# A 3008-point FFT filter ahead of a squared-ReLU FFN: filter loaded as quadrants, zero matmuls in the prologue, two loads of batch 2 later

## The chip, the cores and the metric

The kernel runs on one core of a Trainium2 chip. The metric is the device time of one launch in microseconds (us), the median of three runs. Beside it one execution was profiled, and all rows below are of that execution. [...]

## The reference

```python
X = np.fft.rfft(x, axis=1)                 # x: 8 batches x 3008 rows x 256 columns
F = (filt_r + 1j * filt_i)[None, :, :]     # 1505 frequencies x 256 columns
y = np.fft.irfft(X * F, n=3008, axis=1)    # 8 x 3008 x 256
h = np.maximum(y.reshape(24064, 256) @ w_in, 0.0)    # w_in: 256 x 2048
out = h * h @ w_out                                  # w_out: 2048 x 256
```

All inputs and the output are f32.

## The kernel before

A 3008-point transform is split as 64 x 47. For each batch there are four stages. Stage A (`unit_a`, for batch 0 `chunk_a0`) multiplies by the 47-point matrix; its result u goes through DRAM (`dU`, written in four chunks by `write_u`, read back by `read_u` as the tile ut) so that rows change places. Stage B (`unit_b`, 12 units of two of the 24 columns c) multiplies by `sSB` into psB, and VectorE multiplies psB with the filter sF into prod. Stage P (`unit_p`) multiplies by `sSP` (for batch 0 also by `sSPx`, sSP with its halves exchanged), ScalarE copies the result to ze, and four writes take it to DRAM (`dZ`). Stage Y (`read_z`, then 16 `unit_y`) reads it back as zt and makes yt, the columns of y. The FFN runs over 47 groups of 512 rows, each of 8 slots; a slot has four 512-wide matmuls (`ffn_g1`, psH, ReLU to h on ScalarE L402), the square on VectorE (`ffn_sq`, L406) and eight 256-wide matmuls of the group before (`ffn_g2`, psO).

The order of the work is the order of the program text on every engine and every DMA queue (`manual_schedule`); a DMA issued by an engine stands in that engine's order, and what waits holds back all that follows on the same engine or queue. Batches 1 to 7 are laid between the FFN slots by `fft_plan(b)`: `put(r, place, ...)` puts a step into slot r of the batch's plan, after the first (place 0) or the second (place 1) set of matmuls. For batch 1 the plan's slot 0 is FFN slot 0. Batch 0 is the prologue and has no FFN to lie beside.

In the prologue SP issues three loads of x (L184, 1 MB each), the filter (L193, two loads of 1.5 MB), sSB and sSP (L197, L199), and later ut and the two weight matrices (`load_w`). ACT issues the writes of u and ze, the reads of zt and the first two loads of batch 1. POOL issues no DMA. The tile of each filter part has 128 partitions: quadrant q (32 partitions) holds 12 of the 24 columns, and quadrants 0 and 3 together are the first half of the columns, 1 and 2 the second. `cast_f(im, q, engine)` casts a quadrant into sF, and `cross_f(im, k)` copies or negates half k across partitions on VectorE. The tiles of u have three buffers (`p_u`), so the copies of the fourth chunk of batch 0 (L289, L291) wait until the first chunk's write has landed.

The order of the prologue is L468 to L514: casts of x, four chunks of stage A, ut, weights, casts of the filter, copies of sSPx on POOL, crosses, then 12 turns of stages B and P, casts of the weights on POOL (`cast_w`), reads of zt, stage Y. The FFN begins after it. The filter's load before is

```python
src = bass.AP(tensor=filt.tensor, offset=filt.offset,
              ap=[[12 * D, 4], [47 * D, 32], [1, 12 * D]])
nc.sync.dma_start(out=t, in_=src)
```

whose outermost dimension has 4 entries.

Of the kernel before, what the change touches and what calls it, by code (L numbers as in the profile page):

```python
# [9 lines left out]
F16 = mybir.dt.float16  # L10
F32 = mybir.dt.float32
# [85 lines left out]
def kernel(  # L97
# [9 lines left out]
    nc = tc.nc  # L107
    B, S, D = x.shape
# [13 lines left out]
    const = ctx.enter_context(tc.tile_pool(name="const", bufs=1))  # L122
# [10 lines left out]
    p_y = ctx.enter_context(tc.tile_pool(name="p_y", bufs=2))  # L133
# [12 lines left out]
    def psO(name):  # L146
        return pps.tile([128, 2, 256], F32, tag="psO", name=name, bufs=2)

    def psH(name):
        return pps.tile([128, 2, 512], F32, tag="psH", name=name, bufs=2)  # L150
# [27 lines left out]
    x0 = []  # L178
    v0 = xrows[0:2048, :].rearrange("(p m) d -> p m d", m=16)
    v1 = xrows[2048:3072, :].rearrange("(p m) d -> p m d", m=8)  # L180
    for k, v in enumerate((v0[:, 0:8, :], v1, v0[:, 8:16, :])):
        t = (p_h2 if k == 2 else p_x32).tile([128, 8, D], F32, tag="h2" if k == 2 else "x32",
                                             name=f"x0_{k}")
# [1 line left out]
        x0.append(t)  # L185


    f32s = []
    for k, filt in enumerate((filt_r, filt_i)):
        t = p_y.tile([128, 12, D], F32, tag="yt", name=f"f32_{k}")  # L190
        src = bass.AP(tensor=filt.tensor, offset=filt.offset,
                      ap=[[12 * D, 4], [47 * D, 32], [1, 12 * D]])
        nc.sync.dma_start(out=t, in_=src)  # L193
        f32s.append(t)

    sSB = const.tile([128, NC, 128], F16, name="sSB")
    nc.sync.dma_start(out=sSB, in_=dSB.ap().rearrange("p (a b) -> p a b", b=128))  # L197
    sSP = const.tile([128, NC, 128], F16, name="sSP")
    nc.sync.dma_start(out=sSP, in_=dSP.ap().rearrange("p (a b) -> p a b", b=128))  # L199


    sF = const.tile([128, 2, NC, D], F16, name="sF")

    def cast_f(im, q, eng):

        o = 64 * im + 32 * (q // 2)
        c0 = (0, 12, 12, 0)[q]
        src = f32s[im][32 * q:32 * q + 32, :, :]
        if q >= 2:
            src = src[:, ::-1, :]  # L210
        dst = sF[o:o + 32, im, c0:c0 + 12, :]
        if eng is nc.scalar:
            eng.mul(out=dst, in_=src, mul=-1.0 if im else 1.0)  # L213
        elif im:
            eng.tensor_scalar_mul(out=dst, in0=src, scalar1=-1.0)
        else:
            eng.tensor_copy(out=dst, in_=src)

    def cross_f(im, k):
        c = slice(12 * k, 12 * k + 12)  # L220
        if im:
            nc.vector.tensor_scalar_mul(out=sF[0:64, 1, c, :], in0=sF[64:128, 1, c, :],  # L222
                                        scalar1=-1.0)
        else:
            nc.vector.tensor_copy(out=sF[64:128, 0, c, :], in_=sF[0:64, 0, c, :])  # L225
# [5 lines left out]
    def load_w():  # L231
        w32 = p_h2.tile([128, 2, DFF], F32, tag="h2", name="win32")
        nc.sync.dma_start(out=w32, in_=moe_w_in.rearrange("(t r) j -> r t j", r=128))
        o32 = p_h2.tile([128, NJT, 256], F32, tag="h2", name="wout32")
        nc.sync.dma_start(out=o32, in_=moe_w_out.rearrange("(jt r) c -> r jt c", r=128))
        w32s.extend([w32, o32])

    def cast_w():
        w32, o32 = w32s
        for k in range(4):  # L240
            nc.gpsimd.tensor_copy(out=sWin[:, :, 512 * k:512 * k + 512],
                                  in_=w32[:, :, 512 * k:512 * k + 512])
        for k in range(4):
            nc.gpsimd.tensor_copy(out=sWout[:, 4 * k:4 * k + 4, :], in_=o32[:, 4 * k:4 * k + 4, :])
# [30 lines left out]
    def chunk_a0(c):  # L275

        us[(0, c)] = p_u.tile([96, 8, D], F16, tag="u", name=f"u_0_{c}")
        for k in range(2):
            ps = psH(f"psA_0_{c}_{k}")
            for i in range(2):  # L280
                m = slice(4 * k + 2 * i, 4 * k + 2 * i + 2)
                nc.tensor.matmul(ps[0:96, i, :], s0[:, c // 2, :], x016[2 * (c % 2)][:, m, :],
                                 start=True, stop=False)
                nc.tensor.matmul(ps[0:96, i, :], s0[0:120, 2 + c, :], x016[1][0:120, m, :],
                                 start=False, stop=True)
            o = us[(0, c)][:, 4 * k:4 * k + 4, :]
            pv = ps[0:96].rearrange("p t (a d) -> p (t a) d", d=D)
            if k == 0:
                nc.scalar.copy(out=o, in_=pv)  # L289
            else:  # L290
                nc.vector.tensor_copy(out=o, in_=pv)  # L291
        write_u(0, c, nc.scalar)

    def read_u(b):
        ut = p_ut.tile([128, NC, D], F16, tag="ut", name=f"ut_{b}")
        v = dU[b].rearrange("(p s) d -> p s d", s=NC)
        for s0, s1 in ((0, 8), (8, 24)):
            nc.sync.dma_start(out=ut[:, s0:s1, :], in_=v[:, s0:s1, :])
        uts[b] = ut
# [27 lines left out]
    def unit_p(b, p):  # L327
        c, i6 = divmod(p, 3)
        if i6 == 0:
            zes[(b, c)] = p_ze.tile([128, 6, D], F16, tag="ze", name=f"ze_{b}_{c}")  # L330
        prod = prods.pop((b, p))
        ps = psO(f"psP_{b}_{p}").rearrange("p a d -> p (a d)") if prologue[0] else psF(f"psP_{b}_{p}")
        for i in range(2):
            c2 = 2 * p + i
            if b == 0:
                for v, w in enumerate((sSP, sSPx[0])):
                    nc.tensor.matmul(ps[:, i * D:(i + 1) * D], w[:, c2, :], prod[:, v, i, :],
                                     start=(v == 0), stop=(v == 1))
            else:
                nc.tensor.matmul(ps[:, i * D:(i + 1) * D], sSP[:, c2, :], prod[:, i, :],  # L340
                                 start=True, stop=True)
        nc.scalar.copy(out=zes[(b, c)][:, 2 * i6:2 * i6 + 2, :],  # L342
                       in_=ps.rearrange("p (a d) -> p a d", d=D))
        if i6 == 2:
            q = nc.scalar if prologue[0] else nc.sync
            q.dma_start(
                out=dZ[b].rearrange("(p s) d -> p s d", s=NC)[:, 6 * c:6 * c + 6, :],
                in_=zes.pop((b, c)))
# [76 lines left out]
    def fft_plan(b):  # L425

        plan = {}

        def put(r, place, f, *a):
            plan.setdefault((r, place), []).append((f, a))  # L430

        if b == 1:
            for c in range(2):
                put(c, 1, cast_x, b, c)
                put(c, 1, load_x, b, c + 2)
                put(5 + 2 * c, 1, cast_x, b, c + 2)
        for a in range(16):
            r = 2 + a // 2 + (a >= 8) if b == 1 else a // 2
            put(r, a % 2, unit_a, b, a)
        put(11 if b == 1 else 8, 1, read_u, b)  # L440
        for p in range(12):
            r = 15 + p if b == 1 else 13 + 19 * p // 11
            put(r, 0, unit_b, b, p)
            put(r + (b == 1), b == 1, unit_s, b, p)
            put(r + 2 + (b == 1), 1, unit_p, b, p)
        for c in range(4):
            put(30 if b == 1 else 35, 1, read_z, b, c)
        if b + 1 < B:
            for c in range(2):
                put(22, 1, load_x, b + 1, c)  # L450
            for c in range(4):
                put(27 + 3 * c, 1, cast_x, b + 1, c)
                if c < 2:
                    put(27 + 3 * c, 1, load_x, b + 1, c + 2)
        for n in range(16):
            if b == 1:
                r, k = divmod(n, 3) if n < 6 else divmod(n - 2, 2)
                put(33 + r, min(k, 1), unit_y, b, n)
            else:
                put(39 + n // 2, n % 2, unit_y, b, n)  # L460
        return plan
# [18 lines left out]
        cast_x0(2, i, nc.scalar.copy)  # L480
    chunk_a0(1)
    chunk_a0(3)
    read_u(0)
    load_w()
    for q in (0, 3):
        cast_f(0, q, nc.scalar)
    for q in (1, 2):
        cast_f(0, q, nc.gpsimd)
    for q in (0, 3):
        cast_f(1, q, nc.vector)  # L490
    for q in (1, 2):
        cast_f(1, q, nc.scalar)

    sSPx.append(p_x32.tile([128, NC, 128], F16, tag="x32", name="sSPx"))
    for k in range(2):
        c = slice(12 * k, 12 * k + 12)
        nc.gpsimd.tensor_copy(out=sSPx[0][0:64, c, :], in_=sSP[64:128, c, :])
        nc.gpsimd.tensor_copy(out=sSPx[0][64:128, c, :], in_=sSP[0:64, c, :])
    for k in range(2):
        for im in range(2):  # L500
            cross_f(im, k)
    for r in range(14):
        if r < 12:
            unit_b(0, r)
        if r >= 2:
            unit_p(0, r - 2)
    cast_w()
    for c in range(4):
        read_z(0, c)
# [1 line left out]
        load_x(1, c, q=nc.scalar)  # L511
    for n in range(16):
        unit_y(0, n)
    prologue[0] = False  # L514

    work = {}
# [5 lines left out]
    for s in range((NG + 1) * SLOTS):  # L522
        g, k = divmod(s, SLOTS)
# [40 lines left out]
```

## Time and profile before

| | us |
|---|---|
| runs | 852.3, 854.63, 855.31; median 854.63 |
| the profiled execution's own time | 851.58 |
| its span (first to last instruction) | 849.5 |
| PE busy in the span | 770.7 (91%) |
| DVE, ACT, POOL busy | 552.1, 553.9, 40.6 |
| first matmul of the FFN (L398) | at 97.69 |

Times in rows are microseconds from the span's start. PE is TensorE's matmuls, PEld its weight loads, DVE VectorE, ACT ScalarE, POOL GpSimd, SP the queue engine that issues most DMAs; "SPq" and "ACTq" mark DMA issues. Batch 0 fills the first 97 us, and nothing of the FFN can run before it; from about 190 us on, TensorE is busy all the time.

### The profile page before, as it was taken

The numbers are of one execution on the slowest core, as the hardware profiler recorded it, in microseconds if no ns is written. First come the engines' busy times: TensorE is split into PE (matmuls) and PEld (weight loads), VectorE is DVE, ScalarE is ACT, GpSimd is POOL, SyncE is SP. The second block draws the span as 40 slices with busy tenths as digits, with TensorE's granted clock in tenths as the row PEclk, the third lists the DMA queues.
The fourth block names the chain that finished last, engine by engine and source line by source line (L and its number), as shares of the span: only waits on it lengthen the run. The fifth ranks groups of instructions, "written<-read, shape, count | busy, mean of one in ns | idle before, by whom it ended". The sixth has DMA issues, their size and how long they took to land.

```text
span 849.5 us, 13895 instructions
## 1 busy us (share of the span) xinstructions
PE 770.7 (91%) x5800; PEld 538.7 (63%) x5800; DVE 552.1 (65%) x862; ACT 553.9 (65%) x697; POOL 40.6 (5%) x42
## 2 busy tenths in 40 slices
PE   3105699899999999999999999999999999999998
PEld 1003356566767766677677767677777767676666
DVE  2028479655996579855995579755995579544332
ACT  2035476667777767777777767776777767766664
POOL 0215006200000000000000000000000000000000
PEclk9557599989999999999999999999999999999999
DMA  9328955545455245815455235815454242511111
GB/s 269 96 91 328 221 173 157 135 102 152 144 140 149 81 131 142 204 57 174 125 144 137 82 130 149 208 61 168 129 144 123 81 144 81 130 35 42 38 38 50
DMA packets 89366, 110.10 MB, mean 130 GB/s; under 512 B 3936, under 2 KB 79328, under 8 KB 84704
## 3 DMA queue, kind: packets, MB, share of 16 engines
q1 hardware_dynamic: 82088, 102.71, 41.6%
q10 hardware_dynamic: 7216, 6.51, 3.0%
q8 instruction: 45, 0.74, 0.4%
q14 instruction: 17, 0.14, 0.1%
HBM read 59.40 MB, written 49.81 MB: 129 GB/s over the span
## 4 chain that ended last, share of the span: by engine, by line
PE 84%; DMA 7%; DVE 4%; issue 2%; ACT 2%; ACTq 0%; SPq 0%; DVEq 0%
PE psO L413 38%; PE psH L398 37%; DMA dU<-u 5%; PE psA L264 3%; PE psY L368 2%; PE psB L304 2%; PE psP L340 2%; DVE prod L307 2%; DMA zt<-dZ 1%; DMA x<-in_x_dram 1%; ACT h L402 1%; ACT sF L213 1%; DVE yf L322 0%; DVE sF L225 0%; DVE sF L222 0%
## 5 line engine op out<-in xcount | busy, mean ns | idle before, releaser
L402 ACT ACTIVATE h<-psH 128x1024 f16<-128x1024 f32 x376 | 385.1, 1025 | 191.9 <-PE psH L398 190.4
L398 PE MATMUL psH<-yt,sWin 128*128 128x512 f16 (+7 forms) x1728 | 389.7, 354 | 0.4 <-ACT yt L375 0.2
L413 PE MATMUL psO<-sWout,h 128*128 128x256 f16 x3008 | 390.0, 273 | 0.0
L413 PEld LDWEIGHTS <-h 128*128 128x128 f16 x3008 | 291.4, 98 | 77.8 <-issue 0.6
L406 DVE TENSOR_TENSOR h<-h 128x1024 f16<-128x1024 f16 x376 | 258.9, 697 | 107.6 <-ACT h L402 107.2
L398 PEld LDWEIGHTS <-sWin 128*128 128x128 f16 x1728 | 160.3, 98 | 102.9 <-issue 4.8
L307 DVE TENSOR_TENSOR prod<-psB,sF 128x1024 f16<-128x1024 f32 x96 | 116.1, 1219 | 4.1 <-PE psB L304 3.3
L304 PE MATMUL psB<-ut,sSB 128*128 128x256 f16 x192 | 37.9, 281 | 47.5 <-DMA ut<-dU 41.9
L377 DVE CAST yt<-psY 128x376 f16<-128x376 f32 x64 | 35.2, 550 | 68.1 <-PE psY L368 67.8
L342 ACT CAST ze<-psP 128x512 f16<-128x512 f32 x96 | 56.2, 585 | 28.7 <-PE psP L340 17.8
L271 DVE CAST u<-psA 96x512 f16<-96x512 f32 x56 | 38.4, 686 | 47.8 <-PE psA L264 47.7
L304 PEld LDWEIGHTS <-sSB 128*128 128x128 f16 x192 | 19.2, 100 | 71.0 <-DMA sSB<-cSB 33.8
L420 ACT COPY ost<-psO 128x512 f32<-128x512 f32 x94 | 55.4, 590 | 6.7 <-PE psO L413 6.0
L368 PEld LDWEIGHTS <-zt 96*128 96x128 f16 x512 | 36.5, 105 | 27.9 <-DMA zt<-dZ 13.9
L368 PE MATMUL psY<-sC,zt 96*128 96x94 f16 x512 | 43.2, 217 | 12.0 <-DMA zt<-dZ 12.0
L264 PE MATMUL psA<-x,sC 94*96 94x512 f16 x112 | 42.3, 382 | 0.8 <-ACT u L269 0.6
L375 ACT CAST yt<-psY 128x376 f16<-128x376 f32 x64 | 29.9, 468 | 15.6 <-PE psY L368 15.6
L322 DVE TENSOR_TENSOR yf<-prod,yf 128x512 f16<-128x512 f16 x84 | 35.5, 423 | 3.0 <-POOL yf L316 0.5
L251 DVE CAST x<-x 94x2048 f16<-94x2048 f32 x28 | 34.1, 1217 | 2.1 <-DMA x<-in_x_dram 2.1
L289 ACT CAST u<-psA 96x1024 f16<-96x1024 f32 x4 | 4.0, 1007 | 44.6 <-DMA dU<-u 32.3
L269 ACT CAST u<-psA 96x512 f16<-96x512 f32 x56 | 32.2, 574 | 0.0
L340 PE MATMUL psP<-yf,sSP 128*128 128x256 f16 x168 | 32.1, 273 | 0.0
(31 smaller groups left out, 185.6 us busy)
## 6 DMA issues: line engine op xcount, KB each, us to landing
out_dram<-ost SPq DMA_DIRECT2D x94, 256.0 KB, 3.8
x<-in_x_dram SPq DMA_DIRECT2D x22, 768.0 KB, 5.8
dU<-u SPq DMA_DIRECT2D x28, 384.0 KB, 3.5
dZ<-ze SPq DMA_DIRECT2D x28, 384.0 KB, 2.5
zt<-dZ SPq DMA_DIRECT2D x28, 384.0 KB, 5.4
ut<-dU SPq DMA_DIRECT2D x8, 1024.0 KB, 5.9
ut<-dU SPq DMA_DIRECT2D x8, 512.0 KB, 3.7
x<-in_x_dram SPq DMA_DIRECT2D x3, 1024.0 KB, 8.1
```

The costliest lines, as they stand in the source:

```text
L264: nc.tensor.matmul(ps[0:96, :], sSA, x16s[(b, c)][:, 2 * i:2 * i + 2, :], start=True, stop=True)
L271: nc.vector.tensor_copy(out=o, in_=pv)
L304: nc.tensor.matmul(ps[:, i * D:(i + 1) * D], sSB[:, 2 * p + i, :], uts[b][:, 2 * p + i, :], start=True, stop=True)
L307: nc.vector.tensor_mul(out=prod, in0=ps.rearrange("p (a d) -> p a d", d=D).unsqueeze(1).to_broadcast([128, 2, 2, D]), in1=sF[:, :, 2 * p:2 ...
L340: nc.tensor.matmul(ps[:, i * D:(i + 1) * D], sSP[:, c2, :], prod[:, i, :], start=True, stop=True)
L342: nc.scalar.copy(out=zes[(b, c)][:, 2 * i6:2 * i6 + 2, :], in_=ps.rearrange("p (a d) -> p a d", d=D))
L368: nc.tensor.matmul(ps[:, 94 * jj:94 * jj + 94], zt[:, 4 * (g % 2) + jj, dt * 128:(dt + 1) * 128], sSY, start=True, stop=True)
L398: nc.tensor.matmul(ps[:, i, o:o + n], sWin[:, dt, jt * 128:(jt + 1) * 128], yts[b][:, dt, r:r + n], start=(dt == 0), stop=(dt == 1))
L402: nc.scalar.activation(out=h2[:, 2 * s:2 * s + 2, :], in_=ps, func=AF.Relu)
L406: nc.vector.tensor_mul(out=v, in0=v, in1=v)
L413: nc.tensor.matmul(pso[g][:, t % 2, :], h2s[g][:, jt, t * 128:(t + 1) * 128], sWout[:, jt, :], start=(jt == 0), stop=(jt == NJT - 1))
L420: nc.scalar.copy(out=ost, in_=pso[g])
```

## The change

The filter is loaded as eight quadrant loads of 32 partitions, 384 KB each, whose outermost dimension has 32 entries. Quadrants 0 go on SP where the whole loads stood, quadrants 3 on POOL behind a copy of one element per partition from the second tile of x, quadrants 1 on SP behind the reads of ut, and quadrants 2 on POOL. `keep_warm(n)` issues n matmuls of 128x512 zeros on zeros: 14 ahead of stage A, 50 behind it, 24 ahead of stage Y and two behind every second unit of stage Y. The casts of the second half of the filter move behind the first turns of stages B and P: two on POOL behind the copies of sSPx, two on ACT in turns 2 and 4, and the two crosses of the second half into turn 4. In the plan of batch 1, the four casts of batch 2's x move from slots 27, 30, 33, 36 to 31, 33, 35, 37, and its last two loads from slots 27 and 30 to 31 and 33.

```diff
--- before.py
+++ after.py
@@ -185,18 +185,35 @@
         x0.append(t)
 
 
-    f32s = []
-    for k, filt in enumerate((filt_r, filt_i)):
-        t = p_y.tile([128, 12, D], F32, tag="yt", name=f"f32_{k}")
-        src = bass.AP(tensor=filt.tensor, offset=filt.offset,
-                      ap=[[12 * D, 4], [47 * D, 32], [1, 12 * D]])
-        nc.sync.dma_start(out=t, in_=src)
-        f32s.append(t)
-
+    f32s = [p_y.tile([128, 12, D], F32, tag="yt", name=f"f32_{k}") for k in range(2)]
+
+    def load_f(im, q, eng):
+        filt = filt_i if im else filt_r
+        src = bass.AP(tensor=filt.tensor, offset=filt.offset + 12 * q * D,
+                      ap=[[47 * D, 32], [1, 12 * D]])
+        eng.dma_start(out=f32s[im][32 * q:32 * q + 32].rearrange("p a d -> p (a d)"), in_=src)
+
+    load_f(0, 0, nc.sync)
+    load_f(1, 0, nc.sync)
     sSB = const.tile([128, NC, 128], F16, name="sSB")
     nc.sync.dma_start(out=sSB, in_=dSB.ap().rearrange("p (a b) -> p a b", b=128))
     sSP = const.tile([128, NC, 128], F16, name="sSP")
     nc.sync.dma_start(out=sSP, in_=dSP.ap().rearrange("p (a b) -> p a b", b=128))
+
+    nc.gpsimd.tensor_copy(out=f32s[0][96:128, 0, 0:1], in_=x0[1][96:128, 0, 0:1])
+    load_f(0, 3, nc.gpsimd)
+    load_f(1, 3, nc.gpsimd)
+
+
+    zero = const.tile([128, 512], F16, name="zero")
+    nc.vector.memset(zero, 0.0)
+
+    def keep_warm(n, y=False):
+        ps = psH("warm")[:, 0, :] if y else psO("warm").rearrange("p a d -> p (a d)")
+        for _ in range(n):
+            nc.tensor.matmul(ps, zero[:, 0:128], zero, start=True, stop=True)
+
+    keep_warm(14)
 
 
     sF = const.tile([128, 2, NC, D], F16, name="sF")
@@ -449,9 +466,10 @@
             for c in range(2):
                 put(22, 1, load_x, b + 1, c)
             for c in range(4):
-                put(27 + 3 * c, 1, cast_x, b + 1, c)
+                r = 31 + 2 * c if b == 1 else 27 + 3 * c
+                put(r, 1, cast_x, b + 1, c)
                 if c < 2:
-                    put(27 + 3 * c, 1, load_x, b + 1, c + 2)
+                    put(r, 1, load_x, b + 1, c + 2)
         for n in range(16):
             if b == 1:
                 r, k = divmod(n, 3) if n < 6 else divmod(n - 2, 2)
@@ -480,30 +498,38 @@
         cast_x0(2, i, nc.scalar.copy)
     chunk_a0(1)
     chunk_a0(3)
+    keep_warm(50)
     read_u(0)
+    for im in range(2):
+        load_f(im, 1, nc.sync)
     load_w()
     for q in (0, 3):
         cast_f(0, q, nc.scalar)
-    for q in (1, 2):
-        cast_f(0, q, nc.gpsimd)
     for q in (0, 3):
         cast_f(1, q, nc.vector)
-    for q in (1, 2):
-        cast_f(1, q, nc.scalar)
+    for im in range(2):
+        cross_f(im, 0)
+    for im in range(2):
+        load_f(im, 2, nc.gpsimd)
 
     sSPx.append(p_x32.tile([128, NC, 128], F16, tag="x32", name="sSPx"))
     for k in range(2):
         c = slice(12 * k, 12 * k + 12)
         nc.gpsimd.tensor_copy(out=sSPx[0][0:64, c, :], in_=sSP[64:128, c, :])
         nc.gpsimd.tensor_copy(out=sSPx[0][64:128, c, :], in_=sSP[0:64, c, :])
-    for k in range(2):
-        for im in range(2):
-            cross_f(im, k)
+    for q in (1, 2):
+        cast_f(0, q, nc.gpsimd)
     for r in range(14):
         if r < 12:
             unit_b(0, r)
         if r >= 2:
             unit_p(0, r - 2)
+        if r in (2, 4):
+            cast_f(1, r // 2, nc.scalar)
+        if r == 4:
+            cross_f(0, 1)
+            cross_f(1, 1)
+    keep_warm(24, True)
     cast_w()
     for c in range(4):
         read_z(0, c)
@@ -511,6 +537,8 @@
         load_x(1, c, q=nc.scalar)
     for n in range(16):
         unit_y(0, n)
+        if n % 2:
+            keep_warm(2, True)
     prologue[0] = False
 
     work = {}
```

## Rows read from the trace of the kernel before

**Rows 1.** Stretches: length, PE, PEld, DVE, ACT, POOL busy (count), clock, DMA share, GB/s.

```profile
0.00:10.00 10.00, 0.58 (x1) 0.31 (x2) 1.99 (x4) 1.28 (x1) 0.20 (x4) 1.00 0.83 307
...
30.00:40.00 10.00, 0.00 (x0) 0.00 (x0) 0.00 (x0) 0.00 (x0) 2.42 (x1) 0.50 0.25 87
...
90.00:100.00 10.00, 8.04 (x70) 5.84 (x71) 5.14 (x9) 4.12 (x9) 0.00 (x0) 0.50 1.11 235
...
200.00:400.00 200.00, 200.00 (x1548) 141.93 (x1547) 145.37 (x240) 143.97 (x185) 0.00 (x0) 1.00 0.48 134
```

**Rows 2.** Who waited for whom up to 130 us: total, times, longest.

```profile
PE psB L304 <- DMA ut<-dU: 41.9, 1, 41.9
POOL sF L217 <- DMA f<-in_filt_r_dram: 37.1, 1, 37.1
...
PEld L368 <- DMA zt<-dZ: 9.0, 4, 7.4
```

**Rows 3.** The chain that ended last: start, length, what.

```profile
14.55 38.93 DMA dU<-u
...
69.15 1.94 DVE prod L307 x2
...
88.28 7.69 DMA zt<-dZ
...
97.69 5.12 PE psH L398 x12
...
105.12 0.88 PE psH L398 x4
...
169.00 1.71 PE psO L413 x8
...
176.05 0.87 PE psO L413 x8
```

**Rows 4.** Groups by line, 50 to 90 us: busy us, mean ns, idle before.

```profile
L307 DVE TENSOR_TENSOR prod<-psB,sF 128x1024 f16<-128x1024 f32 x12 | 13.8, 1218 | 0.0
L213 ACT ACTIVATE sF<-f 32x3072 f16<-32x3072 f32 x4 | 11.0, 2760 | 2.5 <-issue 2.4
...
L342 ACT CAST ze<-psP 128x512 f16<-128x512 f32 x12 | 7.0, 586 | 9.1 <-PE psP L337 9.0
...
L497 POOL COPY sSPx<-sSP 64x1536 f16<-64x1536 f16 x2 | 3.5, 1768 | 17.1 <-DMA sSP<-cSP 17.0
L215 DVE TENSOR_SCALAR sF<-f 32x3072 f16<-32x3072 f32 x2 | 3.5, 1754 | 1.1 <-DMA f<-in_filt_i_dram 1.0
L225 DVE COPY sF<-sF 64x3072 f16<-64x3072 f16 x2 | 3.4, 1714 | 3.2 <-ACT sF L213 3.1
L222 DVE TENSOR_SCALAR sF<-sF 64x3072 f16<-64x3072 f16 x2 | 3.1, 1529 | 0.1
...
L291 DVE CAST u<-psA 96x1024 f16<-96x1024 f32 x1 | 1.2, 1221 | 30.7 <-DMA dU<-u 30.7
```

**Rows 5.** Instructions in order of time, 0 to 60 us.

```profile
24.23 0.38 PE L284 MATMUL psA<-x,sC 120*96 120x512 f16 x1
37.58 5.51 POOL L217 CAST sF<-f 32x3072 f16<-32x3072 f32 x2 [37.14 <-DMA f<-in_filt_r_dram]
```

**Rows 6.** DMA issues by line (page, part 6): count, KB, median us to landing.

```profile
x<-in_x_dram SPq DMA_DIRECT2D x22, 768.0 KB, 5.8
dU<-u SPq DMA_DIRECT2D x28, 384.0 KB, 3.5
dZ<-ze SPq DMA_DIRECT2D x28, 384.0 KB, 2.5
...
ut<-dU SPq DMA_DIRECT2D x8, 512.0 KB, 3.7
```

**Rows 7.** Instructions in order of time, SP's queue and PE, 155 to 170 us.

```profile
157.12 0.33 SPq L163 DMA_DIRECT2D x<-in_x_dram  x1
...
159.23 0.32 SPq L346 DMA_DIRECT2D dZ<-ze  x1
164.56 2.38 SPq L353 DMA_DIRECT2D zt<-dZ  x4
...
168.50 0.50 PE L368 MATMUL psY<-sC,zt 96*128 96x94 f16 x4 [3.85 <-DMA zt<-dZ]
```

## The prediction, made before the changed kernel ran

> **What bounds the kernel now.** I began with busy time by stretch [rows 1]. From 200 to 400 us TensorE is busy 200 of 200 us at clock 1.00: nothing in this change makes the FFN itself shorter. In the prologue it is the other way round: between 30 and 40 us no engine but POOL does anything (2.42 us), the DMA engines are busy 0.25 and move 87 GB/s, against 0.83 and 307 GB/s in the first 10 us. A quarter of 16 engines is four, and the filter's load has 4 as its outermost dimension. So the prologue waits for two transfers of 1.5 MB that use four DMA engines.
>
> The waits say who suffers [rows 2]: POOL waits 37.1 us for the filter, and TensorE 41.9 us for ut. The chain shows why ut is late too [rows 3]: the write of the first chunk of u is issued at 14.55 and lands 38.93 us later, where the same write takes 3.5 us at the median later on [rows 6]. It lies behind the filter on those four engines. The last matmul of stage A ran at 24.23 [rows 5], but the copy of its result had to wait 30.7 us [rows 4] for the buffer that this write holds. ut is there only at 24.6 + 41.9 = 66.5, the first product comes at 69.15, the 12 products take 13.8 us [rows 4], to 82.9, and the FFN begins at 97.69 [rows 3]. What the prologue loses, the end loses: the FFN that follows is full.
>
> **The change part by part.** *ut.* The first loads, with 128 outermost, kept 0.83 of the engines busy [rows 1]; with 32 outermost I take a quadrant to spread over all 16. Rate: 307 GB/s at a share of 0.83 [rows 1] is 370 GB/s for a full share. Ahead of or beside the writes of u lie constants and x (3.4 MB), six quadrants (2.4 MB, those on POOL among them) and sSB and sSP (1.6 MB): 7.3 MB, 20 us, so drained at about 21. Stage A's matmuls end at 24.6 [rows 5]; some 16 of them ran at 1.2 GHz, worth 0.427 - 0.22 = 0.21 us each (5.12 / 12 and 0.88 / 4 [rows 3]), 3.4 us if all are at 2.4 GHz. With the last copy (1.22 [rows 4]) the last write is issued at 22.5 to 26; I take 23, since the 14 zero matmuls, 6 us even at 0.427, end at about 7, before the first cast of x. The fill of the zero tile on DVE and the small copy on POOL lie in the wait for x; only POOL's loads stand behind that copy. It lands 3.5 later [rows 6], at 26.5, and the first part of ut 3.7 after that [rows 6], at 30.2.
>
> *First half of the filter.* On ACT, behind the last chunk, two casts of 2.76: 23.4 to 28.9; on DVE two of 1.75 beside them, then crosses of 1.71 and 1.53 [rows 4]: 32.2. TensorE runs 50 zero matmuls from about 21.5; at 0.22 they end at 32.5. First product about 33, instead of 69.15: the zero matmuls and the crosses end it together, and ut is no longer what is late.
>
> *Second half.* Five products of 1.22 [rows 4] end at 39.1; there DVE waits for the crosses of the second half, and everything behind them on DVE with it. Quadrants 1 stand behind ut on SP: 1.57 + 0.79 MB from 26.6 at 370 GB/s, and 1 us to land, 34. POOL, done with its copies of sSPx by then (four of 1.77 [rows 4]), casts two quadrants in 5.5 [rows 5]: 39.5. ACT casts in turns 2 and 4, with ze copies of 0.59 between them [rows 4]: first ze at 35.5, then 2.76, two ze, 2.76: 42.2. That cast decides; a cross of 1.53 behind it, 43.7, and seven products of 1.22: 52.2, instead of 82.9. So 30.7 us less, of which the new wait has already taken some 4.6 back.
>
> *Behind it.* The weights' loads start some 35 us earlier on SP, 4.2 MB behind quadrants 1 land by 34 + 11.3 = 45.5, before the products end; their casts on POOL stay hidden. The 24 zero matmuls take 5.3 us at 0.22 and 10.3 at 0.427; they lie in the wait for the first zt (7.4 at the longest [rows 2]), and at the slow clock they overlap with the later zt, of which the chain waits 7.69 us [rows 3]. Two between pairs of units lie in the same wait (9.0 in four pieces in all [rows 2]). So I cost them at nothing; without that cover they would cost up to 5 + 3.5 us. The time from the last product to the FFN stays at 97.69 - 82.9 = 14.8: the FFN begins at about 67, 31 us earlier.
>
> *Clock at the FFN's start.* 90 to 100 us ran at 0.50 [rows 1]: 12 matmuls took 5.12 instead of 2.64 [rows 3]. But these first slots also wait for batch 1's x, which is not earlier relative to them. Gain between 0 and 4; I take 1.
>
> *Batch 2's loads.* At 157.12 SP issues a load of x, at 159.23 the last write of ze behind it; it has landed only when the reads of zt are issued at 164.56 [rows 7], 5.3 later instead of 2.5 [rows 6]. TensorE waits 3.85 us for zt [rows 7] and is then at the lower clock: eight matmuls 1.71, at full clock 0.87 [rows 3]. The slow stretch reaches from 168.5 to somewhere before 176.05; I take 5.8 us of it, of which half, 2.9, is lost. With the load behind the reads, zt comes 2.8 earlier; the wait falls to about 1, and a wait that short need not cost the clock: 2.8 + 2.2 = 5. The end on the good side is 3.85 + 2.9 = 6.7. On the other side the moved load itself may come late: issued at about 164.4, behind four zt, it could land at 174, and its cast is due in slot 35, about 170. DVE would wait up to 4 us, of which TensorE has about 3 in hand (1.5 slots of 2.08 until it needs the buffer that DVE empties). So the range is 6.7 gained to 1 lost; I take 5, because such a load lands in 5.8 at the median [rows 6], in time for its cast.
>
> Sum: 31 + 1 + 5 = 37 us. Against the profiled execution's own 851.58 that is 814.6. The median of the runs shown is 854.63, 3.05 above it, so I forecast 817.6.
>
> **The rivals.**
> *The zero matmuls stand in the way.* TensorE is in order. If the 50 run at 1.2 GHz throughout, they take 21.4 and end at 43; the first product comes at 43.5, five more end at 49.6, the crosses (3.2) at 52.8, seven at 61.3, the FFN at 76.1, 21.6 earlier. With 6 of the other parts: 827. For it: the clock was 0.50 from 30 us on [rows 1]. Against it: where the FFN's matmuls follow one another from 97.69 on, the step from 0.427 to 0.22 us came before 105.12 [rows 3].
>
> *Quadrants are no faster.* If what limits the filter is not the four engines but these long rows themselves, six quadrants (2.4 MB) need 27 us at 87 GB/s [rows 1], from 10 to 37; the writes of u land with them at about 39, ut at 44, quadrants 1 at 53, ACT's second cast at 56.5, the cross at 58, the last product at 66.6, the FFN at 81.4: 16.3 earlier, with 6 for the rest 832. [...]
>
> *POOL's queue becomes the bound.* This is the case on the other side. POOL issues no load before, so no row has its price. Four quadrants, the sSPx copies, two casts and all casts of the weights now stand in line there. If its loads go pair behind pair and each takes what the slowest transfer of this prologue took (38.93 [rows 3]), quadrants 3 land at 49, quadrants 2 at 88; casts end at 93.5, the cross at 95.2, seven products at 103.7, the FFN starts at 118.5, 20.8 later than now; with 6 gained elsewhere 869. It decides from the point at which POOL's second cast ends after 77, against 39.5 in my working; between 71 and 83 or so the time would be as before.
>
> **How the numbers follow.** My forecast gets 0.76. Its own range is 807 (the products follow ut directly, clock and batch 2 at their better ends: 36 + 4 + 6.7) to 825 (28 us in all: quadrants and writes some 6 us later, batch 2's loads for nothing). The zero matmuls in the way 0.09, at 827; quadrants no faster 0.10, at 832; POOL 0.05. The range is 807 to 832, which leaves out POOL and the edges of the others. Half a per cent, 4.3 us, is about what a measurement of this kernel can tell from no change. Faster by more than that: all but POOL's case, 0.95. POOL's case splits into 0.02 for about the same and 0.03 for slower.
>
> **What would show it.** The DMA share between 10 and 25 us near 1 and no stretch at 0.25; writes of u landing within 10 us; the first product (L307) at about 33 and a hole of some 4 us in them ahead of the crosses of the second half, ended by ACT; the last product at about 52, the first FFN matmul at about 67; the reads of batch 1's zt about 2.8 us earlier relative to the FFN's start, and no half-clock stretch behind them. I am wrong if the first product waits for ut or a zero matmul beyond 38, if POOL's casts are what DVE waits for, or if the FFN's start moves by less than 22 us.

## The result, and the profile after

The changed kernel takes 828.62 us (median of 4 runs, 827.2 to 829.61) against 854.37 (852.3 to 855.31) for the kernel before: ratio 0.9701 [0.9675, 0.9726], 25.7 us faster. The forecast was 817.6 with a range of 807 to 832: the range holds it, and of the 37 us forecast some 11 did not come. The profiled execution took 829.54, its span is 827.8 (849.5 before). This execution is one of the slower of its four, and that of before was the fastest of all, so the rows differ by 22 us and the medians by 25.7.

Stretches of the kernel after, columns as in [rows 1]:

```profile
10.00:20.00 10.00, 5.88 (x23) 3.00 (x23) 2.90 (x3) 5.01 (x5) 2.08 (x4) 0.93 1.05 279
20.00:30.00 10.00, 10.00 (x44) 4.56 (x43) 3.07 (x3) 1.22 (x2) 2.58 (x2) 0.90 0.97 262
30.00:40.00 10.00, 4.97 (x26) 2.40 (x25) 9.36 (x6) 5.31 (x2) 6.12 (x3) 0.95 0.80 252
```

The stretch at a DMA share of 0.25 is gone. But between 10 and 30 us, at shares of 1.05 and 0.97, the DMA engines move only 279 and 262 GB/s, not the 370 of the forecast. The first waits have shrunk as foreseen; a view of who waited for whom up to 130 us (total, times, longest), to lay beside [rows 2]:

```profile
ACT u L306 <- DMA dU<-u: 8.4, 1, 8.4
...
POOL sF L234 <- DMA f<-in_filt_r_dram: 5.4, 1, 5.4
...
PE psB L321 <- DMA ut<-dU: 2.8, 1, 2.8
```

The 41.9 us for ut are 2.8 (the 50 zero matmuls, which end at 33.8, fill the rest of this wait), the 37.1 of POOL are 5.4. The chain that ended last (start, length, what) beside [rows 3]:

```profile
12.95 15.05 DMA dU<-u
...
29.43 3.26 DMA dU<-u
...
34.06 9.43 DMA f<-in_filt_i_dram
...
68.58 12.53 DMA x<-in_x_dram
...
84.19 1.71 PE psH L415 x4
```

The first write of u still holds the chain, for 15.05 us instead of 38.93. Then comes a piece that before did not have, 9.43 us for a quadrant of the filter; and the FFN's first slots wait for x of batch 1. Instructions of the kernel after in order of time (start, length, engine, line; in brackets the idle time before and what ended it):

```profile
27.38 1.46 POOL L518 COPY sSPx<-sSP 64x1536 f16<-64x1536 f16 x1 [15.09 <-DMA sSP<-cSP]
28.08 1.01 ACT L306 CAST u<-psA 96x1024 f16<-96x1024 f32 x1 [8.38 <-DMA dU<-u]
29.37 5.52 DVE L232 TENSOR_SCALAR sF<-f 32x3072 f16<-32x3072 f32 x2
36.60 0.60 PE L321 MATMUL psB<-ut,sSB 128*128 128x256 f16 x4 [2.82 <-DMA ut<-dU]
37.06 0.95 DVE L239 TENSOR_SCALAR sF<-sF 64x3072 f16<-64x3072 f16 x1
38.12 5.75 DVE L324 TENSOR_TENSOR prod<-psB,sF 128x1024 f16<-128x1024 f32 x5
43.51 2.76 ACT L230 ACTIVATE sF<-f 32x3072 f16<-32x3072 f32 x1 [2.04 <-DMA f<-in_filt_i_dram]
47.20 0.95 DVE L242 COPY sF<-sF 64x3072 f16<-64x3072 f16 x1 [3.33 <-POOL sF L234]
47.78 2.76 ACT L230 ACTIVATE sF<-f 32x3072 f16<-32x3072 f32 x1 [0.42 <-ACT ze L359]
50.58 1.64 DVE L239 TENSOR_SCALAR sF<-sF 64x3072 f16<-64x3072 f16 x1 [2.42 <-ACT sF L230]
52.25 8.25 DVE L324 TENSOR_TENSOR prod<-psB,sF 128x1024 f16<-128x1024 f32 x7
76.34 1.92 PE L415 MATMUL psH<-yt,sWin 128*128 128x512 f16 x8
```

Five products start at 38.12. Where the twelve of [rows 4] follow one another, there is now a hole from 43.87 to 52.25; the last product ends at 60.50, and the FFN begins at 76.34: 21.35 us earlier than in [rows 3], not 31. What the first product waited for last was not ut, whose psB began at 36.60, but a cross on VectorE (37.06 to 38.01). The casts ahead of that cross began only at 29.37, behind the copy that had waited for the first write of u, and VectorE's two took 5.52 us instead of the 3.5 of [rows 4].

Batch 2, the same view, beside [rows 7]:

```profile
139.54 0.32 SPq L363 DMA_DIRECT2D dZ<-ze  x1
141.98 2.37 SPq L370 DMA_DIRECT2D zt<-dZ  x4
...
145.70 0.34 PE L385 MATMUL psY<-sC,zt 96*128 96x94 f16 x4 [0.74 <-DMA zt<-dZ]
...
153.47 1.22 DVE L268 CAST x<-x 94x2048 f16<-94x2048 f32 x1 [2.79 <-DMA x<-in_x_dram]
158.07 1.22 DVE L268 CAST x<-x 94x2048 f16<-94x2048 f32 x1 [1.26 <-DMA x<-in_x_dram]
...
166.92 4.74 SPq L272 DMA_DIRECT2D dU<-u  x2
```

The reads of zt follow the last write of ze by 2.4 us, before by 5.3; TensorE waits 0.74 instead of 3.85. The last write of ze at 139.54 is 19.69 earlier than in [rows 7]; the first write of u of batch 3, at 166.92, is 24.06 earlier than before's, which is this row of its queue:

```profile
190.98 4.73 SPq L255 DMA_DIRECT2D dU<-u  x2
```

So the difference of the two spans adds up as 21.35 at the FFN's start, less 1.66 in its first slots, plus 4.37 around batch 2, less 2.36 in small steps later that I did not follow: 21.7.

### The profile page after: what moved, and what is told of

It reads as the page before. It is cut to its first block, busy times and chain, and to the rows that moved or that the text cites. A ratio compares the mean times of both kernels' runs of the same rounds, so it can differ in the third digit from the quotient of the medians.

```text
span 827.8 us, 14116 instructions
## 1 busy us (share of the span) xinstructions
PE 791.7 (96%) x5904; PEld 546.6 (66%) x5904; DVE 553.2 (67%) x863; ACT 553.7 (67%) x697; POOL 45.7 (6%) x47
## 4 chain that ended last, share of the span: by engine, by line
PE 83%; DMA 9%; DVE 3%; issue 2%; ACT 1%; ACTq 1%; SPq 0%; DVEq 0%
PE psO L430 37%; PE psH L415 36%; DMA x<-in_x_dram 4%; PE psA L281 3%; PE psB L321 2%; DMA dU<-u 2%; PE psY L385 2%; PE psP L357 2%; DMA f<-in_filt_i_dram 1%; DMA zt<-dZ 1%; DVE prod L324 1%; DMA dZ<-ze 1%; ACT h L419 1%; DVE h L423 1%; PE psP L354 0%
## 5 line engine op out<-in xcount | busy, mean ns | idle before, releaser
L385 PEld LDWEIGHTS <-zt 96*128 96x128 f16 x512 | 34.8, 99 | 23.5 <-DMA zt<-dZ 6.7
L385 PE MATMUL psY<-sC,zt 96*128 96x94 f16 x512 | 41.5, 207 | 4.7 <-DMA zt<-dZ 3.7
L392 ACT CAST yt<-psY 128x376 f16<-128x376 f32 x64 | 29.9, 468 | 11.8 <-PE psY L385 11.7
L214 PE MATMUL warm<-zero 128*128 128x512 f16 x104 | 27.2, 412 | 1.2 <-DVE zero L209 1.2
```

Of the source, the lines that this page charges most:

```text
L385: nc.tensor.matmul(ps[:, 94 * jj:94 * jj + 94], zt[:, 4 * (g % 2) + jj, dt * 128:(dt + 1) * 128], sSY, start=True, stop=True)
```

## The experiments

**The load's outermost dimension alone.** The kernel before, two dimensions of one access pattern exchanged:

```diff
-                      ap=[[12 * D, 4], [47 * D, 32], [1, 12 * D]])
+                      ap=[[47 * D, 32], [12 * D, 4], [1, 12 * D]])
```

> The kernel before, with the first two dimensions of the filter's load exchanged: still two loads of 128 partitions on SP, but 32 outermost instead of 4. It changes which filter row lies on which partition, so the products use other coefficients; the work is the same. Theory A (four DMA engines were what held the filter, and u behind it): no stretch at a DMA share of 0.25 is left; x ends at about 11.3 us, 3.15 MB of filter at some 400 GB/s end at 20, sSB and sSP at 24; the writes of u land by 30, the first product (L307) comes at about 39, the FFN's first matmul at about 68 instead of 97.69, the time is about 825 (820 to 830). Theory B (the long rows are slow whatever the engines): the filter is there no earlier than 50 us, and the time stays within 5 us of 854.

Measured: 821.9 us (820.91 to 824.19), ratio 0.966 [0.9618, 0.9702]. In time this line alone is worth at least as much as the whole change. What it leaves out is the place of the rows: they now lie on other partitions, so the products use other coefficients, and a version that reads them where they lie was not run. Its stretch and its products:

```profile
10.00:20.00 10.00, 6.26 (x15) 2.71 (x14) 2.58 (x3) 2.73 (x3) 4.91 (x2) 1.00 1.01 425
...
27.66 11.09 ACT L213 ACTIVATE sF<-f 32x3072 f16<-32x3072 f32 x4 [1.35 <-DVE u L291]
34.34 1.01 PE L304 MATMUL psB<-ut,sSB 128*128 128x256 f16 x4 [8.44 <-DMA ut<-dU]
39.77 13.67 DVE L307 TENSOR_TENSOR prod<-psB,sF 128x1024 f16<-128x1024 f32 x12
68.16 4.64 PE L398 MATMUL psH<-yt,sWin 128*128 128x512 f16 x12 [0.25 <-ACT yt L375]
```

At about the same busy share the engines move 425 GB/s, not 279, and ut is there at 34.34 instead of 36.60. The first product is 1.65 us later than in the kernel after, since ACT makes four casts in a row ahead of it, but all twelve follow one another, and the FFN begins at 68.16.

**The quadrants alone.** The kernel before with eight loads of 32 partitions, all on SP, in the old place:

```diff
-        t = p_y.tile([128, 12, D], F32, tag="yt", name=f"f32_{k}")
-        src = bass.AP(tensor=filt.tensor, offset=filt.offset,
-                      ap=[[12 * D, 4], [47 * D, 32], [1, 12 * D]])
-        nc.sync.dma_start(out=t, in_=src)
+        for q in range(4):
+            src = bass.AP(tensor=filt.tensor, offset=filt.offset + 12 * q * D,
+                          ap=[[47 * D, 32], [1, 12 * D]])
+            nc.sync.dma_start(out=f32s[k][32 * q:32 * q + 32].rearrange("p a d -> p (a d)"), in_=src)
```

> The kernel before, with each filter part loaded as four quadrants of 32 partitions, all eight on SP in the place of the two loads; nothing else. Theory A (16 engines, but half the rate per byte into 32 partitions): the filter takes 3.15 MB at 200 GB/s, from 11 to 27, where the two loads with the rows first took until 18 at 430 GB/s; sSB and sSP end at 31, the writes of u land by 35, the first product comes at 44 to 45, the FFN 7 to 9 us later than there; time about 830. Rival F (the half rate came only from two queues side by side): as fast as the load with the rows first, 820 to 824.

Measured: 822.77 us (821.1 to 823.38), ratio 0.9649 [0.9623, 0.9675]; 830 was a miss. The time is the rival's, but not for its reason: a single queue moves as little as the two of the kernel after. The low rate costs little:

```profile
10.00:20.00 10.00, 6.63 (x15) 2.84 (x15) 2.91 (x3) 2.36 (x3) 3.77 (x2) 1.00 1.02 238
...
14.52 8.50 SPq L193 DMA_DIRECT2D f<-in_filt_i_dram  x4
...
39.25 1.01 PE L303 MATMUL psB<-ut,sSB 128*128 128x256 f16 x4 [12.55 <-DMA ut<-dU]
...
40.64 13.67 DVE L306 TENSOR_TENSOR prod<-psB,sF 128x1024 f16<-128x1024 f32 x12
69.51 4.59 PE L397 MATMUL psH<-yt,sWin 128*128 128x512 f16 x12 [0.25 <-ACT yt L374]
```

Some writes of u lie in that stretch. From 12 to 14 us, where neither kernel has issued one, the rates for the quadrants and then for rows first are

```profile
12.00:14.00 2.00, 1.06 (x3) 0.41 (x2) 0.90 (x1) 0.40 (x1) 0.00 (x0) 1.00 0.99 203
```

```profile
12.00:14.00 2.00, 0.73 (x2) 0.20 (x1) 1.22 (x1) 0.07 (x1) 0.00 (x0) 1.00 1.01 430
```

The two kernels differ only in how the filter's load is cut, so pieces of 32 partitions and 384 KB moved at half the rate of loads of 128 partitions and 1.5 MB (203 against 430 GB/s); no run separates the partitions from the size. SP issued the second part's loads only from 14.52 on, one by one, and the first write of u, issued at 14.41, took 7.2 us instead of 15.05; I take it that it found a gap between them. The price of the slow quadrants shows in ut, for which TensorE waits until 39.25, 4.9 us longer than with rows first; ACT's four casts, 28.45 to 39.56, and a cross behind them end only 1.4 us later, so these set the first product here as they do with rows first, 0.9 us behind it.

**The quadrant as 4 by 8 rows**, to hold it on four engines:

```diff
-                      ap=[[47 * D, 32], [1, 12 * D]])
+                      ap=[[47 * D * 8, 4], [47 * D, 8], [1, 12 * D]])
```

> The changed kernel, with each quadrant's load written as 4 x 8 rows, so that 4 is outermost again; split, queues, order and zero matmuls stay. Theory A (the number of engines): the loads of quadrants 0 and 3 take two to four times as long as in the changed kernel (13 and 20 us from issue to landing there), the first write of u lands at 33 or later instead of 28, and the time rises by 5 to 20 us over 828.6, to 834 to 848. Theory B (the split and the two queues brought the gain): within 2 us of 828.6.

Measured: 830.34 us in one run. Its loads landed much as those of the kernel after (7.8 to 17.1 us from issue, against 7.9 to 15.3; DMA share 1.03 from 10 to 30 us), so they were not held to four engines. The two dimensions name the same addresses in the same order as one of 32, and I take it that they were joined to that before the load ran; no run shows it. If so, it repeats the changed kernel and tells nothing of the number of engines.

**No zero matmuls.** The kernel after without its four calls of `keep_warm`:

```diff
-    keep_warm(14)
...
-    keep_warm(50)
...
-    keep_warm(24, True)
...
-        if n % 2:
-            keep_warm(2, True)
```

> The changed kernel without any of the zero matmuls. Theory A (the prologue waits for DMA, and the clock is on its path only in short pieces): the first write of u is issued some 1.5 us later but still lands at 28, stage Y runs without its extra matmuls, the FFN's first slots are at the lower clock but wait for x of batch 1 anyhow; the time is within 2.5 us of 828.6. Rival C (the clock is a real part of the gain): slower by 5 us or more, 833 to 838.

Measured: 826.71 us (826.28 to 829.63), ratio to before 0.972 [0.9678, 0.9762], no different from the change itself. In its order of instructions:

```profile
38.35 5.75 DVE L323 TENSOR_TENSOR prod<-psB,sF 128x1024 f16<-128x1024 f32 x5
...
76.53 4.69 PE L414 MATMUL psH<-yt,sWin 128*128 128x512 f16 x12 [0.25 <-ACT yt L391]
90.08 1.04 PE L429 MATMUL psO<-sWout,h 128*128 128x256 f16 x8
```

First product 0.23 us later, FFN 0.19 later, while the first psO comes at 90.08, earlier than the 91.81 of the kernel after. Stage A's first write of u went out at 14.44 instead of 12.95, and that bought nothing: the copies of the fourth chunk wait for that write until 28 either way.

**Batch 2's loads alone.** The kernel before with the two plan lines of the change:

```diff
-                put(27 + 3 * c, 1, cast_x, b + 1, c)
+                r = 31 + 2 * c if b == 1 else 27 + 3 * c
+                put(r, 1, cast_x, b + 1, c)
...
-                    put(27 + 3 * c, 1, load_x, b + 1, c + 2)
+                    put(r, 1, load_x, b + 1, c + 2)
```

> The kernel before with only the casts and loads of batch 2 moved. By the changed trace this edit is worth the difference between the lead of the slots before slot 32 (19.7 us) and after slot 40 (24.1 us), so 4.4 us: 850 against 854.4, reads of batch 1's zt issued 2.5 us earlier, no stretch at the lower clock behind them. Rival: it gains only behind the shorter prologue, and the time is 854.

Measured: 848.21 us (10 runs, 843.01 to 851.48) against 851.76, ratio 0.9957 [0.9927, 0.9987]. Its queue:

```profile
157.68 0.32 SPq L346 DMA_DIRECT2D dZ<-ze  x1
160.16 2.44 SPq L353 DMA_DIRECT2D zt<-dZ  x4
185.72 4.74 SPq L255 DMA_DIRECT2D dU<-u  x2
```

Ahead of the edit it runs 1.55 us before [rows 7] (157.68 against 159.23), which the edit cannot have made; behind it 5.26 (185.72 against 190.98). By rows the edit is worth 3.7 us here (3.6 between the medians), 4.4 in the kernel after.

**Casts in the order in which the quadrants arrive.** The kernel after; quadrants 2, there since 27 us, cast ahead of quadrants 1:

```diff
-    for q in (1, 2):
+    for q in (2, 1):
         cast_f(0, q, nc.gpsimd)
+    cast_f(1, 2, nc.scalar)
...
-        if r in (2, 4):
-            cast_f(1, r // 2, nc.scalar)
+        if r == 2:
+            cast_f(1, 1, nc.scalar)
```

> The changed kernel, with the casts of quadrants 2, which are there at 27, ahead of those of quadrants 1, which land at 43.5: on POOL in the order 2, 1, on ACT the one of quadrant 2 ahead of the 12 turns. Theory A (the second half waits for quadrant 1, and both casts of ACT stand behind that wait): ACT's cast of quadrant 2 falls into its idle time at 35.4, the one of quadrant 1 runs from 43.5 to 46.3, POOL is done at 44.4; the second set of products starts at about 47.3 instead of 52.3, the FFN 5 us earlier, time 824. Rival D (the ze copies or POOL set it): the start of the second set moves by less than 2 us, time 827 to 829.

Measured: 824.07 us (2 runs), ratio 0.9665 [0.9605, 0.9726]:

```profile
40.90 5.75 DVE L324 TENSOR_TENSOR prod<-psB,sF 128x1024 f16<-128x1024 f32 x5
46.67 0.95 DVE L242 COPY sF<-sF 64x3072 f16<-64x3072 f16 x1
47.66 0.96 DVE L239 TENSOR_SCALAR sF<-sF 64x3072 f16<-64x3072 f16 x1
48.65 8.01 DVE L324 TENSOR_TENSOR prod<-psB,sF 128x1024 f16<-128x1024 f32 x7
71.36 1.92 PE L415 MATMUL psH<-yt,sWin 128*128 128x512 f16 x8
```

Though the first five products start 2.8 us later, the crosses of the second half follow them without a wait, and the FFN begins 5.0 earlier. The first five start later because DVE's cross took 3.38 us beside a cast on POOL instead of 0.95. So the order of the casts cost the change some 5 us. That is read from one trace; between the medians of 2 and 4 runs it is some 4.5 us, and the intervals of the two ratios overlap.

**What holds ut.** Three more variants of the kernel after looked for the 5 us by which the first product was late. A fourth buffer for u:

```diff
-        us[(0, c)] = p_u.tile([96, 8, D], F16, tag="u", name=f"u_0_{c}")
+        us[(0, c)] = (p_zt if c == 3 else p_u).tile([96, 8, D], F16, tag="zt" if c == 3 else "u",
+                                                    name=f"u_0_{c}")
```

> The changed kernel, with the fourth chunk of u in a buffer of the tag zt, so that its copies wait for no write. Theory A (the writes of u get hardly any share while other queues hold loads, up to 26, and then run at full rate): the last write is issued at about 23.5 instead of 29.4 and the four land together at about 30.5 instead of 32.7; first product at 36 instead of 38.1; time about 826.5. Rival E (a write of u takes 15 us whenever it is issued): the last one lands at 38, and the time rises by 4 us or more.

Measured: 828.3 us (2 runs). The last write of u is issued at 28.12 instead of 29.43, but the first part of ut lands at 36.94, where the kernel after has its psB at 36.60, and the first product is at 38.28, behind a cross on DVE that took 2.10 us. The fourth chunk no longer waits for the buffer, but ut's reads are issued 3.82 us after the last write of u instead of 3.68, and DVE's two casts and two crosses beside POOL's copies take 5.83, 1.98 and 2.10 us instead of 5.52, 1.67 and 0.95. POOL's second pair of loads held back behind two of its copies:

```diff
-    for im in range(2):
-        load_f(im, 2, nc.gpsimd)
...
+        if k == 0:
+            nc.gpsimd.tensor_copy(out=f32s[0][64:96, 0, 0:1], in_=sSPx[0][64:96, 0, 0:1])
+            for im in range(2):
+                load_f(im, 2, nc.gpsimd)
```

> The changed kernel, with POOL's loads of quadrants 2 issued only behind the first two copies of sSPx. Theory A (loads in other queues hold back the writes of u): 0.79 MB less lies beside them, 4 us at the 200 GB/s of a quadrant; the first write of u lands at about 24 instead of 28, ut 3.5 earlier, first product at 34.6; quadrants 1 and 2 come together at about 39, the second set of products starts at 47 to 48 instead of 52.3; time 823 to 825. Rival E (the write takes 15 us by itself): it still lands at 28, quadrants 2 come later, time 829 or more.

Measured: 829.36 us (2 runs). The third write of u, with little beside it, was there after 3.2 us; the fourth then ran beside the loads that had been held, and

```profile
26.86 10.96 PE L214 MATMUL warm<-zero 128*128 128x512 f16 x50
37.65 0.60 PE L321 MATMUL psB<-ut,sSB 128*128 128x256 f16 x4
```

here the zero matmuls end TensorE's wait, with no idle time between them and psB, while the first part of ut landed at 37.4: the cost moved and nothing was gained. And quadrants 1 on SP straight behind quadrants 0:

```diff
     load_f(1, 0, nc.sync)
+    load_f(0, 1, nc.sync)
+    load_f(1, 1, nc.sync)
```

> The changed kernel, with quadrants 1 loaded on SP directly behind quadrants 0, ahead of sSB and sSP. [...] Rival F (quadrants go at half the rate on any two queues): the first write lands at 32, first product at 42, time within 1 us of 828.6 or slower.

Measured: 829.4 us (2 runs). Now sSP stood behind them and was issued only at 30.08; ut's reads went out at 37.03, the first product started at 41.38, and the second set at 52.81, behind ACT's casts, no earlier than 52.25. From 10 to 30 us its DMA engines moved 245 GB/s, those of the kernel after 271. None of the three brings ut forward. The first two miss the times first expected of them (826.5, 823 to 825); the third is within 1 us of 828.6, as its rival has it. From the issue of the last write of u to that of ut's reads passed 3.7 us in the kernel after, and 3.8, 5.0 and 5.5 in these three.

**Versions.** The better parts together in the kernel after (no zero matmuls, the fourth buffer, quadrants 1 on ACT's queue, casts in order of arrival, one load of batch 1's x earlier):

```diff
-        load_f(im, 1, nc.sync)
+        load_f(im, 1, nc.scalar)
...
+    cast_f(1, 2, nc.scalar)
+    load_x(1, 0)
...
-    for c in range(2):
-        load_x(1, c, q=nc.scalar)
+    load_x(1, 1, q=nc.scalar)
```

> A version put together from the runs: the changed kernel without zero matmuls, with the fourth chunk of u in a buffer of the tag zt, quadrants 1 loaded on ACT's queue behind the last write of u instead of on SP behind ut, the casts of quadrants 2 ahead of those of quadrants 1, and the first load of batch 1's x on SP ahead of the 12 turns. Theory A: the last write of u lands at about 31, quadrants 1 at 38 instead of 43.5, the second set of products starts at 43 to 45 instead of 52.3, the first FFN matmul comes at 67 to 69 instead of 76.3 and its first slots wait less for x; time 815 to 819. If something else sets the prologue, the sum of the parts does not come: 824 or more, no better than the casts in the other order alone.

Measured: 823.65 us (822.16 to 825.48), ratio 0.9666 [0.9641, 0.9691]; 815 to 819 was a miss. The first product started at 40.12: DVE's two casts took 5.65 us and its crosses up to 3.38 beside POOL's copies and casts. Then the quadrants on SP together with batch 2's plan, in the kernel before, nothing else (the diff of the quadrants alone and that of batch 2's loads alone, above):

> The kernel before with two edits alone: the eight quadrant loads on SP in the old place, and the casts and loads of batch 2 in their new slots. No zero matmuls, no second queue, no filter loads behind ut, no casts in the turns. If the two edits add (28.7 us and 4.4 us by slots), 818 (816 to 820), some 9 us faster than the whole change; if the changed kernel's other parts carry gain that these lack, 824 or more.

Measured: 819.36 us (6 runs, 818.39 to 820.49) against 850.79, ratio 0.9627 [0.96, 0.9654], as expected if the two edits add. It beats both kernels; its interval lies below that of the change, [0.9675, 0.9726]. Last, the same with one of ACT's four casts on DVE and a load of batch 1's x earlier on SP:

```diff
-    for q in (1, 2):
-        cast_f(1, q, nc.scalar)
+    cast_f(1, 1, nc.vector)
+    cast_f(1, 2, nc.scalar)
...
+    load_x(1, 0)
...
-    for c in range(2):
-        load_x(1, c, q=nc.scalar)
+    load_x(1, 1, q=nc.scalar)
```

> As the version with the two edits, and in it the first load of batch 1's x on SP ahead of the 12 turns, and one of ACT's four filter casts (imaginary part, quadrant 1) on DVE. ACT's casts end 2.8 us earlier, the products start when ut is there, 1.3 us earlier; the FFN's first slots wait less for x, 2 us: 815 (813 to 817). If ut alone sets the first product and the first slots wait for something else, no change against the version with the two edits.

Measured: 820.65 us (820.07 to 822.04), ratio 0.9645 [0.9619, 0.9672]; 815 was a miss. Its order of instructions and its chain:

```profile
36.14 0.95 DVE L221 TENSOR_SCALAR sF<-sF 64x3072 f16<-64x3072 f16 x1
40.38 13.75 DVE L306 TENSOR_TENSOR prod<-psB,sF 128x1024 f16<-128x1024 f32 x12 [3.28 <-PE psB L303]
...
55.45 4.72 DMA dZ<-ze
```

The filter is ready at 37.1, but now ut is late again, and the first product gains only 1.1 us on the 41.52 of the version before; the last write of ze takes 4.72 instead of 2.31, and the FFN begins at 71.09, behind the 69.86 of that version.

## Why the forecast held and where it was wrong

**The range held partly by luck.** The forecast's own case ended at 825 (28 us off 854.63 is in fact 826.6), and 828.62 lies beyond either. The range reached 832 only for two rivals, zero matmuls in the way and quadrants no faster, and the runs refute the cause of both. What follows is where the sum went wrong.

**What bounded the kernel: right.** With the load whose outermost dimension has 4 entries the DMA share was 0.25 [rows 1], and u's first write took 38.93 us beside it [rows 3]. Both kernels that change nothing but the filter's load (rows first, quadrants on SP) remove it: 29.9 and 28.7 us between medians. The rival that quadrants are no faster falls in its cause: rows first keeps the rows as long as they were, and the share goes to 1.0. The limit was the share of the engines, 0.25 against 1.01, and not the long rows; and the split alone gained 28.7 us.

**The step that failed: the rate of the quadrants, and with it the writes of u.** The forecast took 370 GB/s from a stretch of 128-partition loads [rows 1] and had 7.3 MB drained at 21. The rows show 279 and 262 GB/s at a full share for the kernel after, 238 for quadrants on SP, 425 for the load over 128 partitions in the same stretch, and 203 against 430 with no write of u beside them. sSP, the last of the loads, was there at 27.4, and the writes of u, beside loads all that time, took as long: the last was issued at 29.43, not 23. The copy that the first write held back delayed the casts too, and VectorE's were priced at 1.75 us each, from a stretch without POOL's copies beside them, but took 2.76. The first product came at 38.12, not 33: psB began at 36.60, and the crosses ended last, at 38.01. At 203 GB/s the quadrants take 1.8 times the time that I gave them (an estimate, 370 / 203); why pieces of 32 partitions moved at half the rate no run shows.

**Second half of the filter: the hole was foreseen, its size not.** The forecast was 4.6 us between the two sets of products, the measured hole is 8.4 (43.87 to 52.25). Quadrants 1 were issued 7 us late, behind ut, and took 9.43 us instead of 7.4 (no run shows the 1 us for landing in that); and the cast of the one that comes last stood ahead of the cast of one that had long been there. Casting in order of arrival brings the FFN 5.0 us forward in its trace. The last product ends at 60.5 instead of 52.2: this and the step before are 8.3 of the 9.3 us by which the FFN is late (76.34 instead of 67), the rest is the stretch behind the products, 15.8 instead of 14.8.

**Clock at the FFN's start: wrong sign.** Forecast 1 us gained, measured 1.66 lost. Over the first 10 us of the FFN the granted clock did rise, but only from 0.76 to 0.85 (the 0.50 of [rows 1] lies mostly ahead of the FFN), and the first eight psH took 1.92 us. But x of batch 1 is loaded behind the same reads of zt as before and lands at 81.1, so the first slots wait for it, and behind that wait four psH take 1.71 us at a granted clock of 0.50, the pace of the first twelve before [rows 3]. No run gives TensorE's clock in GHz, as the prediction's working does. The traces show a granted share and a pace: before, twelve psH took 0.427 us each at 0.50 and four took 0.22 each at 1.00 [rows 3], but in its stage A matmuls followed one another by 0.43 also at 1.00 (10.43 to 12.56).

**Zero matmuls: right, and worth nothing.** They stood in the way of nothing here (the rival at 827 falls, though its time is the nearest to the measured one), nor did they help: 826.7 without, 828.6 with.

**POOL: right.** Its casts ended at 47.2, later than the 39.5 forecast, and DVE's wait of 3.33 us in the hole was for them; but ACT's, which ended at 50.54, decided. The case on the other side did not come near.

**Batch 2: right, 4.4 for 5.** The wait for zt fell to 0.74, and no half-clock stretch follows it: over the 7.3 us behind it the granted clock is 1.00, where before it was 0.62 from 168.5 to 176. The moved loads came late as the bound on the other side allowed: DVE waits 2.79 and 1.26 us for x.

So the mechanism was right and three terms of the sum were mis-sized: the start of the products, the hole in them, and the first slots. By rows the 31 became 21.35, the 1 a loss of 1.66 and the 5 became 4.37, with 2.36 lost in steps that I did not follow. By its own test, the FFN's start moving by less than 22 us, the forecast is just wrong: 21.35. What the diff adds to the quadrants and the plan (a second queue, zero matmuls, quadrants 1 behind ut, casts in the turns) costs some 6 us together: a ratio of 0.9701 against 0.9627 without it, of 850. The order of the casts alone is worth some 5 of it in its trace; the rest was not taken apart.

## What to carry to other kernels

Look at the outermost dimension of every large transfer and at the DMA share while it runs; a share of 0.25 with everybody waiting was worth one line of code here (29.9 us). A transfer over 128 partitions with many outermost entries moved its bytes at twice the rate of pieces of 32 (430 GB/s against 203), though here the two came to the same time (821.9 and 822.8 us), since casts and not loads set the first product. When a load is cut into pieces, let the work on them follow their order of arrival, and do that before adding queues. Make the simplest edit that removes the bound by itself first: here it beat the version with four more ideas on top.

## What the runs showed of the hardware

In the kernel after, writes of 512-byte rows nearly stood still beside loads in longer ones. From 13 to 25 us ACT's queue, which has three writes of u in it by then, moved 0.07 MB while the loads moved 3.12; from 25 to 28 us, with the loads nearly done, 0.62 MB. The view of transfers from 10 to 30 us gives, for the kernel after, then for rows first, size and median us from issue to landing of u's writes (512-byte rows):

```profile
dU<-u ACTq DMA_DIRECT2D x4, 384.0 KB, 8.4
```

```profile
dU<-u ACTq DMA_DIRECT2D x4, 384.0 KB, 4.5
```

The one of 15.05 us above ended only when the loads of 12 KB rows did; with little beside it one took 3.2.

Loads issued by POOL were slow to come: the first, issued at 10.21, took 9.2 us for 384 KB, and POOL's queue moved no byte until 16 us. The 14 zero matmuls ahead of stage A let its first write go out at 12.95 in the profiled run, but in five other kernels with the same 14 at 13.47 to 14.55, where before has 14.55 [rows 3] and the kernel without them 14.44: the 1.6 us were not to be had for certain. And DVE and POOL were slower when both copied or cast: DVE's casts of a quadrant took 2.76 us each beside POOL's copies of sSPx, and 1.77 with quadrants 1 early, where POOL stood idle then; these copies of POOL took 1.46 or 2.88.
